# Attention in front of a mixture of experts: strided heads in 24 groups of 54 tokens instead of 32 groups of 36

## The chip, the core and the metric

The kernel runs on one core of one Trainium2 chip. The metric is device microseconds of one execution. In the profile PE is TensorE's matmuls, PEld its weight loads, DVE is VectorE, ACT is ScalarE, POOL is GpSimd and SP is SyncE, which issues most transfers here.

## What is computed

Attention over 4 batches, 8 heads, 576 tokens and 64 features per head, followed by a layer of eight experts and by a dense layer (512 to 2048 to 512, with an ELU between). The change touches the attention alone. Heads 0 to 3 look back over a window of 32 tokens; heads 4 to 7 are strided: a token sees the earlier tokens with the same remainder modulo 32.

```python
scores = scale * np.matmul(q, k.transpose(0, 1, 3, 2))
rel = pos[:, None] - pos[None, :]
mask_local = (rel >= 0) & (rel < stride)
mask_strided = (rel >= 0) & (pos[None, :] % stride == pos[:, None] % stride)
scores = np.where(masks[None, :, :, :], scores, -1000000000.0)
attn = np.exp(scores - np.max(scores, axis=-1, keepdims=True))
attn = attn / (np.sum(attn, axis=-1, keepdims=True) + 1e-09)
return np.matmul(attn, v).astype(np.float32)
```

Each of the 32 remainders has 18 tokens, so the tokens that can see each other are small sets, and tokens of several remainders share one block with a mask.

## The kernel before, in words

**Stages.** The attention runs in about the first 120 us; the matmuls of the first expert come in at its end. Then five planned expert jobs and the dense layer fill the rest of the span. Each engine runs its instructions in the order in which the program emits them (`manual_schedule`); the framework adds the waits that the data need, and a tile that reuses a buffer waits for everything that used the tile before it, transfers included.

**Turns.** The attention takes its heads in pairs. For each batch the order is `PAIRS = [2, 0, 3, 1]`: strided, local, strided, local, so that the sixteen pairs n = 0 to 15 alternate. A turn n of the loop at L1425 emits, in this order: `emit_S(n)` (scores, DVE's addition of the mask, DVE's maximum, POOL's subtraction, then `store_x`), the transposes of q and k of pair n + 1 (`emit_T`), `emit_PT(n - 1)` (transposes of the exponentials), more transposes, `emit_PV(n - 1)` (P times V, then DVE's product with the reciprocal sum into the x tile, L1330 for strided and L1358 and L1361 for local heads), `emit_X(n - 2)` (transposes of x, and ACT's copy into xt), after a batch's last pair `emit_L` and `emit_lg` (the router's logits), then `emit_exp(n)`, the loads of q and k of pair n + 3 and of V of pair n + 2. `bg()` places work of the first expert between them.

**Strided pairs.** A group holds 36 tokens: those of two remainders, 16 groups per head. PE multiplies 64 columns of q (36 of them used) with 36 tokens of k for a group in a quarter of its array, and writes eight slots of 36 scores for each half of the partitions and each head. A float32 matmul is two passes, so a pair has 64 of them for scores (L1246) and 64 for P times V (L1326), eight transposes of P (L1285) and eight of x (L1386). V is loaded by two transfers with rows of 2 KB (L1127).

**x tiles.** `x_sb` of a batch is one tile for its two strided pairs (`xs1`) and one for its two local pairs (`xs0`), each with one buffer (L1081). When the second pair of a kind is through (`pr % 2`), its stores to `x_dram` are appended to a list: two for a strided tile (L1338), three for a local one (L1365, 512 KB, and twice L1368, 32 KB). `store_x` at the end of `emit_S` empties the list onto POOL's queue. So the local stores of a batch are issued in turns 5, 9 and 13, and the next batch's first local pair writes the tile in turns 6, 10 and 14:

```python
    def store_x():
        while stores:
            stores.pop(0)()
```

PSUM tiles come from a function `bank` with a tag: S (scores, two banks), T (transposes of q and k, two), P (transposes of P, P times V and transposes of x, four). `idle` is a tile of zeros in bf16.

Of the kernel before, what the change touches and what calls it, by code (L numbers as in the profile page):

```python
# [24 lines left out]
M = 72  # L25
G = 8
J = 36
# [1044 lines left out]
def attention(tc, bg, q, k, v, mod, mbias, wg, x_dram, ident, router, bank):  # L1072
# [16 lines left out]
    vs = [const.tile([128, 2, G, D], F32, name=f"vs{i}") for i in range(2)]  # L1089
    vl = [const.tile([KW, 9, 2, D + 1], F32, name=f"vl{i}") for i in range(2)]  # L1090
    qt = [t_p.tile([128, S + 32], F32, name=f"qt{i}") for i in range(2)]

    kt = [t_p.tile([128, 32 + S], F32, name=f"kt{i}") for i in range(2)]
    sm_s = const.tile([128, 16 * D], F32, name="sm_s")
    sm_l = const.tile([128, 9, KW], F32, name="sm_l")
    pt_s = const.tile([128, 10 * D], F32, name="pt_s")
# [37 lines left out]

    mask_s = const.tile([128, J], F32, name="mask_s")
# [5 lines left out]
    def strided_mask():  # L1141
        di = const.tile([128, J], I32, name="di")
        nc.gpsimd.iota(di, pattern=[[-1, J]], base=64, channel_multiplier=1)
        nc.vector.tensor_scalar(di, di, 1, None, ALU.bitwise_and)
        nc.vector.tensor_copy(mask_s, di)
        nc.vector.tensor_scalar(mask_s, mask_s, NEG, None, ALU.mult)
        for x in range(2):
            sel(mask_s[64 * x:64 * x + 64], -1, ALU.is_ge, 0, 1)
# [17 lines left out]
    for t in qt:  # L1166
        nc.vector.memset(t[:, S:], 0.0)
    strided_mask()
    nc.vector.memset(sm_s, 0.0)
    nc.vector.memset(pt_s[:, S:], 0.0)  # L1170
# [46 lines left out]
    def emit_T(n, j):  # L1217

        b, pr = pairs[n]
        src = (qn if j < 2 else kn)[b, pr]  # L1220
        x = j % 2
        o = qt[n % 2][:, 0:S] if j < 2 else kt[n % 2][:, 32:]
        if pr >= 2:
            ps = bank("T", "ps_tr", 128, 3, 96)
            for c in range(3):
                nc.tensor.transpose(ps[:, c], src[:, 3 * x + c], ident[0:96, 0:96])
            nc.scalar.copy(o.rearrange("p (c w j) -> p c w j", w=2, j=J)[:, 4 * x:4 * x + 4], ps.rearrange("p x m -> p (x m)").rearrange("p (j w c) -> p c w j", w=2, c=4))
        else:
            ps = bank("T", "ps_tr", 128, 3, 96)
            for c in range(3):  # L1230
                nc.tensor.transpose(ps[:, c], src[:, 2 * c + x], ident[0:96, 0:96])
            nc.scalar.copy(o.rearrange("p (c m a) -> p c m a", c=3, a=2)[:, :, :, x], ps)

    def emit_S(n):
# [3 lines left out]
        if strided:  # L1238
            pss = [bank("S", f"ps_sc{r}", 128, 8, J) for r in range(2)]
            for i in range(8):  # L1240
                h, t, y = i // 4, i // 2 % 2, i % 2
                for x in range(2):
                    at = ((4 * h + 2 * x + t) * 2 + y) * J
                    for r in range(2):
                        ro = slice(D * r, D * r + D)
                        nc.tensor.matmul(pss[r][64 * x:64 * x + 64, i], lhsT=q_sb[ro, at:at + 64],  # L1246
                                         rhs=k_sb[ro, 32 + at:32 + at + J], start=True, stop=True)
            sm = sm_s.rearrange("p (s k) -> p s k", k=D)[:, :, 0:J]
            masks = [mask_s.unsqueeze(1).to_broadcast([128, 8, J])] * 2
            parts = [(0, 8), (8, 16)]  # L1250
        else:
            parts = [(0, TAIL + 1), (TAIL + 1, 9)]
            pss = [bank("S", f"ps_sl{r}", 128, TAIL + 1, KW) for r in range(2)]
            for s in range(TAIL + 1):
                for x in range(2):
                    for r in range(2):
                        if s == TAIL and r > x:
                            continue
                        blk = 64 * (2 * s + (x if s < TAIL else 0))
                        ro = slice(D * r, D * r + D)  # L1260
                        nc.tensor.matmul(pss[r][64 * x:64 * x + 64, s], lhsT=q_sb[ro, blk:blk + 64],
                                         rhs=k_sb[ro, blk:blk + KW], start=True, stop=True)
            sm = sm_l
            masks = [mask_l[:, i:j] for i, j in parts]
# [8 lines left out]
        store_x()  # L1273
# [5 lines left out]
    def emit_PT(n):  # L1279
        if pairs[n][1] >= 2:  # L1280
            sm, pt = sm_s, pt_s
            for r in range(2):
                ps = bank("P", "ps_p")
                for g in range(4):
                    nc.tensor.transpose(ps[:, 128 * g:128 * g + 128], sm[:, 512 * r + 128 * g:512 * r + 128 * g + 128], ident)  # L1285
                nc.scalar.copy(pt[:, 8 * J * r:8 * J * (r + 1)].rearrange("p (b q) -> p b q", q=J),
                               ps.rearrange("p (b q) -> p b q", q=D)[:, :, 0:J])
            rs = m_p.tile([128, 16], F32, tag="rs", name="rs")
# [4 lines left out]
            rec = m_p.tile([128, 2, 8], F32, tag="rec", name="rec")  # L1293
            nc.vector.reciprocal(rec.rearrange("p w (g r) -> p r g w", r=2), rs.rearrange("p (r g w) -> p r g w", r=2, w=2))
            bg()
            rss[n] = rec
            return
# [8 lines left out]
    xt = const.tile([128, 4, S], F32, name="xt")  # L1306

    def emit_PV(n):
# [4 lines left out]
        if key not in xs:  # L1313
            sh = [128, 8, 4, D] if strided else [128, 18, D]
            xs[key] = xs_p.tile(sh, F32, tag=f"xs{pr // 2}", name="xs")
        x_sb = xs[key]
        xb = x_dram[b * S:(b + 1) * S]
        if strided:
            pss = [bank("P", "ps_v", 128, 8, D) for w in range(2)]
            for g in range(8):  # L1320
                h, t, r = g // 4, g // 2 % 2, g % 2
                for x in range(2):
                    for w in range(2):
                        ro = slice(64 * w, 64 * w + J)
                        at = (8 * r + 4 * h + 2 * t + x) * J
                        nc.tensor.matmul(pss[w][64 * x:64 * x + 64, g], lhsT=pt_s[ro, at:at + 64],  # L1326
                                         rhs=vs[pr - 2][ro, h, 4 * x + 2 * t + r], start=True, stop=True)
            rec = rss.pop(n).rearrange("p w (h t) -> p w h t", h=2)
            for w in range(2):
                nc.vector.tensor_tensor(x_sb[:, 4 * w:4 * w + 4, h0:h0 + 2].rearrange("p t h d -> p h t d"),  # L1330
                                        pss[w].rearrange("p (h t) d -> p h t d", h=2),
                                        rec[:, w].unsqueeze(3).to_broadcast([128, 2, 4, D]), ALU.mult)
                bg()
                bg()
            if pr % 2:
                o = xb[:, 4 * D:].rearrange("(q w x t) d -> x q w t d", w=2, x=2, t=4)
                for x in range(2):
                    stores.append(lambda x=x: nc.gpsimd.dma_start(o[x], x_sb[64 * x:64 * x + J].rearrange("q (w t) h d -> q w t (h d)", w=2)))  # L1338
# [31 lines left out]
    def store_x():  # L1370
        while stores:
            stores.pop(0)()

    def emit_X(n):
# [4 lines left out]
        if n + 2 >= NP:  # L1379
            store_x()  # L1380
        if pr >= 2:
            for half in range(2):
                ps = bank("P", "ps_x")
                o = ps.rearrange("p (q x t) -> p t x q", x=2, t=4)
                for g in range(4):
                    nc.tensor.transpose(o[:, g], x_sb[:, 4 * half + g, h0:h0 + 2].rearrange("p h d -> p (h d)"), ident)  # L1386
                nc.scalar.copy(xt[:, pr].rearrange("p (q t) -> p q t", q=J)[:, :, 8 * half:8 * half + 8],
                               ps.rearrange("p (q t) -> p q t", t=8)[:, 0:J])
# [7 lines left out]
        nc.scalar.copy(xt[:, pr, 0:512], ps)  # L1396
        nc.scalar.copy(xt[:, pr, 512:S], pe)
# [3 lines left out]
    def emit_L(b):  # L1401

        for half in range(2):
            ps = bank("T", "ps_l", 128, S // 2)
            for kk in range(4):
                nc.tensor.matmul(ps[32 * kk:32 * kk + 32], lhsT=wgp[:, kk], rhs=xt[:, kk, half * (S // 2):(half + 1) * (S // 2)],
# [87 lines left out]
```

## Time and profile before

| | |
|---|---|
| median of three runs | 731.36 us (728.81 to 732.5) |
| the profiled execution's own time | 732.11 us |
| its span, first to last instruction | 730.4 us |
| mean granted clock of TensorE | 0.993 |
| transfers over the span | 127.36 MB, 174 GB/s |

Durations below come from the one profiled execution, whose time is 1.7 us above its span. A busy share is an average over stages that differ: the attention's is read from its own stretch. Idle time of an engine stands in brackets behind a row, with what ended it. Queue rows (PEldq, SPq) are of the sequencers.

### The profile page before, as it was taken

The page shows a single profiled execution, that of the slowest core. Times are in us where ns is not written, and L with a number is a line of the kernel's source. Part 1 is how long each engine was busy: PE and PEld are TensorE (multiplying, and loading weights), DVE is VectorE, ACT ScalarE, POOL GpSimd, SP SyncE. Part 2 cuts the span into 40 slices and gives each one's busy share as a digit, 9 for nine tenths or more (in the row PEclk, how much of TensorE's full clock was granted, in tenths as well). Part 3 has the DMA queues.
Part 4 walks back from the last instruction along what each step waited for, and adds up shares of the span by engine and source line. Part 5 has one row for each costly group of instructions (what it writes and reads, how often), then busy time and mean ns, then how long its engine had stood idle before and what let it go on. Part 6 is the DMA issues. An engine that isn't in the chain of part 4 may idle for free.

```text
span 730.4 us, 13943 instructions
## 1 busy us (share of the span) xinstructions
PE 711.9 (97%) x5263; PEld 626.1 (86%) x5266; DVE 555.0 (76%) x1068; ACT 415.9 (57%) x761; POOL 110.1 (15%) x164
## 2 busy tenths in 40 slices
PE   8899989999999999999999999999999999999996
PEld 5788876888888888888998998999889889899895
DVE  4668876967879877777878867787788898777763
ACT  5577775235544546455555546675565677565643
POOL 3444352121020200000000000021000003200003
PEclk9899999999999999999999999999999999999999
DMA  9988773177586686674865464165433345533302
GB/s 192 196 223 197 209 229 95 61 231 230 163 281 212 210 272 195 202 237 149 292 227 204 172 217 144 58 207 168 165 124 115 116 142 204 189 130 116 115 2 86
DMA packets 94983, 127.36 MB, mean 174 GB/s; under 512 B 19415, under 2 KB 66551, under 8 KB 94912
## 3 DMA queue, kind: packets, MB, share of 16 engines
q1 hardware_dynamic: 85440, 94.91, 42.7%
q0 software_dynamic: 9472, 31.51, 13.0%
q8 instruction: 43, 0.70, 0.4%
q14 instruction: 28, 0.23, 0.1%
HBM read 100.18 MB, written 26.21 MB: 173 GB/s over the span
## 4 chain that ended last, share of the span: by engine, by line
PE 51%; POOL 1%; issue 0%; POOLq 0%; ACT 0%
PE h_ps L719 25%; PE o_ps L810 9%; PE o_ps L809 9%; PE o_ps L808 9%; POOL out_dram L819 1%; POOLq L1490 0%; ACT y_sb L817 0%; POOLq L819 0%
## 5 line engine op out<-in xcount | busy, mean ns | idle before, releaser
L810 PE MATMUL o_ps<-wh,gl 128*128 128x512 f32 x282 | 111.2, 394 | 0.0
L809 PE MATMUL o_ps<-wl,gh 128*128 128x512 f32 x282 | 111.0, 394 | 0.0
L808 PE MATMUL o_ps<-wh,gh 128*128 128x512 f32 x282 | 110.6, 392 | 0.0
L794 ACT CAST gh<-t 128x384 fp32r<-128x384 f32 x94 | 48.3, 514 | 102.3 <-DVE t L746 100.3
L490 DVE TENSOR_TENSOR wl<-wraw,wh 128x1024 fp32r<-128x1024 f32 x56 | 69.0, 1232 | 32.4 <-ACT wh L489 31.9
L719 PE MATMUL h_ps<-xa,wh 128*128 128x384 f32 x320 | 87.6, 338 | 1.1 <-DVEq L756 0.6
L745 DVE SCALAR_TENSOR_TENSOR t<-e,t 128x384 f32<-128x384 f32 x96 | 53.4, 557 | 28.7 <-ACT e L740 26.3
L870 POOL DMA_DIRECT2D wl<-wl_dram x32 | 17.5, 551 | 338.1 <-PE o_ps L810 197.6
L719 PEld LDWEIGHTS h_ps<-xa,wh 128*128 128x128 f32 x320 | 59.3, 188 | 7.8 <-issue 1.6
L800 DVE TENSOR_TENSOR gl<-t,gh 128x384 fp32r<-128x384 f32 x94 | 52.2, 556 | 17.3 <-ACT gh L794 15.5
L719 PE MATMUL h_ps<-xa,wl 128*128 128x384 f32 x192 | 64.6, 336 | 0.0
L810 PEld LDWEIGHTS o_ps<-wh,gl 128*128 128x128 f32 x282 | 52.9, 188 | 12.0
L524 PE MATMUL y_ps<-hh,wh 128*128 128x460 f32 (+1 forms) x160 | 61.4, 384 | 0.0
L526 PE MATMUL y_ps<-hh,wl 128*128 128x460 f32 (+1 forms) x160 | 60.1, 375 | 0.0
L525 PE MATMUL y_ps<-hl,wh 128*128 128x460 f32 (+1 forms) x160 | 60.0, 375 | 0.0
L489 ACT CAST wh<-wraw 128x1024 fp32r<-128x1024 f32 x56 | 58.4, 1043 | 0.0
L809 PEld LDWEIGHTS o_ps<-wl,gh 128*128 128x128 f32 x282 | 53.0, 188 | 6.2
L808 PEld LDWEIGHTS o_ps<-wh,gh 128*128 128x128 f32 x282 | 53.0, 188 | 6.2
L147 ACT ACTIVATE conv<-conv 128x512 f32<-128x512 f32 x32 | 21.8, 681 | 58.8 <-DVE conv L159 58.6
L719 PE MATMUL h_ps<-xb,wh 128*128 128x384 f32 x192 | 54.6, 338 | 0.0
L874 ACT CAST wh<-wraw 128x1024 fp32r<-128x1024 f32 x48 | 50.1, 1043 | 0.0
L719 PE MATMUL h_ps<-xc,wh 128*128 128x384 f32 x192 | 49.3, 338 | 0.0
(270 smaller groups left out, 1589.2 us busy)
## 6 DMA issues: line engine op xcount, KB each, us to landing
wraw<-w_f SPq DMA_DIRECT2D x48, 512.0 KB
wraw<-in_moe_w_dram SPq DMA_DIRECT2D x80, 256.0 KB
wl<-wl_dram POOLq DMA_DIRECT2D x32, 512.0 KB, 4.4
conv<-in_moe_w_in_dram SPq DMA_DIRECT2D x16, 512.0 KB
conv<-in_moe_w_out_dram SPq DMA_DIRECT2D x16, 512.0 KB
w_f<-conv SPq DMA_DIRECT2D x32, 256.0 KB
wl_dram<-wl SPq DMA_DIRECT2D x16, 512.0 KB
qn<-in_q_dram SPq DMA_DIRECT2D x16, 288.0 KB
```

Source lines behind the costliest of these rows:

```text
L489: nc.scalar.copy(WH[i], raw)
L490: nc.vector.tensor_tensor(WL[i], raw, WH[i].bitcast(F32), ALU.subtract)
L524: nc.tensor.matmul(ps, lhsT=a, rhs=hh, start=f == 0, stop=False)
L525: nc.tensor.matmul(ps, lhsT=a, rhs=hl, start=False, stop=False)
L526: nc.tensor.matmul(ps, lhsT=b, rhs=hh, start=False, stop=f == NCH - 1)
L719: mm = lambda x, v, f, l: nc.tensor.matmul(ps, lhsT=x, rhs=v, start=f, stop=l, skip_group_check=on)
L745: nc.vector.scalar_tensor_tensor(t, e, 1.0, t, ALU.add, ALU.mult)
L800: nc.vector.tensor_tensor(gl, t, gh.bitcast(F32), ALU.subtract)
L808: nc.tensor.matmul(ps, lhsT=a, rhs=hi, start=first, stop=False)
L809: nc.tensor.matmul(ps, lhsT=a, rhs=lo, start=False, stop=False)
L810: nc.tensor.matmul(ps, lhsT=b, rhs=hi, start=False, stop=last)
L874: nc.scalar.copy(WH[slots(n)[nm]], wts[n, nm])
```

## The change

`J, R3, Z = 18, 3, 3`, `N3 = J * R3` = 54 and `Q6 = 2 * Z * N3` = 324 replace M, G and the old J. A group holds the tokens of three remainders, 12 groups per head; the last ones reach beyond 32 remainders and hold padding. Scores have six slots of 54 instead of eight of 36 for each head, P and x six slots instead of eight. V of a strided pair is loaded by six transfers of 18 rows each, in pieces of 512 bytes. After the transposes of a strided tile of q or k a matmul with two columns of zeros fills two columns that the copy reads as padding. The strided x tile gets two buffers, the local one keeps one (`bufs=1 + pr // 2`). A strided x tile is stored by six transfers, and `store_x` takes at most how many stores to issue. xt gets rows of 36 with 32 used. The mask is made by POOL alone, and unused rows of V are filled with zeros.

```diff
-M = 72
-G = 8
-J = 36
+J, R3, Z = 18, 3, 3
+N3 = J * R3
+Q6 = 2 * Z * N3
...
-            src = v[b, h:h + 2].rearrange("h (j w a) d -> w j h (a d)", w=2, a=G)
+            src = v[b, h:h + 2].rearrange("h (j c a) d -> h j c (a d)", c=16, a=2)
             for w in range(2):
-                nc.sync.dma_start(vs[pr - 2][64 * w:64 * w + J].rearrange("j h a d -> j h (a d)"), src[w])
+                for i in range(R3):
+                    n = min(6, 16 - 6 * i)
+                    ro = slice(64 * w + J * i, 64 * w + J * (i + 1))
+                    nc.sync.dma_start(vs[pr - 2][ro, 0:n, 0:2 * D], src[w, :, 6 * i:6 * i + n])
...
         if pr >= 2:
-            ps = bank("T", "ps_tr", 128, 3, 96)
+            ps = bank("T", "ps_tr")
             for c in range(3):
-                nc.tensor.transpose(ps[:, c], src[:, 3 * x + c], ident[0:96, 0:96])
-            nc.scalar.copy(o.rearrange("p (c w j) -> p c w j", w=2, j=J)[:, 4 * x:4 * x + 4], ps.rearrange("p x m -> p (x m)").rearrange("p (j w c) -> p c w j", w=2, c=4))
+                nc.tensor.transpose(ps[:, 96 * c:96 * c + 96], src[:, 3 * x + c], ident[0:96, 0:96])
+            nc.tensor.matmul(ps[:, 288:290], lhsT=idle[:, 0:128], rhs=idle[:, 0:2], start=True, stop=True)
+            o = qt[n % 2][:, Q6 * x:Q6 * x + Q6] if j < 2 else kt[n % 2][:, 32 + Q6 * x:32 + Q6 * x + Q6]
+            wide = bass.AP(ps.tensor, ps.offset, [list(ps.ap[0]), [1, 6], [6, R3], [16, J]])
+            nc.scalar.copy(o.rearrange("p (v i j) -> p v i j", i=R3, j=J), wide)
...
-            pss = [bank("S", f"ps_sc{r}", 128, 8, J) for r in range(2)]
-            for i in range(8):
...
+            pss = [bank("S", f"ps_sc{r}", 128, 6, N3) for r in range(2)]
+            for z in range(Z):
+                for h in range(2):
+                    for x in range(2):
+                        at = (6 * h + 3 * x + z) * N3
+                        for r in range(2):
+                            ro = slice(D * r, D * r + D)
+                            nc.tensor.matmul(pss[r][64 * x:64 * x + 64, 2 * z + h], lhsT=q_sb[ro, at:at + 64],
+                                             rhs=k_sb[ro, 32 + at:32 + at + N3], start=True, stop=True)
...
-        store_x()
+        store_x(3)
...
-                for g in range(4):
-                    nc.tensor.transpose(ps[:, 128 * g:128 * g + 128], sm[:, 512 * r + 128 * g:512 * r + 128 * g + 128], ident)
...
+                for z in range(Z):
+                    nc.tensor.transpose(ps[:, 128 * z:128 * z + 128], sm[:, 384 * r + 128 * z:384 * r + 128 * z + 128], ident)
...
-            sh = [128, 8, 4, D] if strided else [128, 18, D]
-            xs[key] = xs_p.tile(sh, F32, tag=f"xs{pr // 2}", name="xs")
+            sh = [128, 6, 4, D] if strided else [128, 18, D]
+            xs[key] = xs_p.tile(sh, F32, tag=f"xs{pr // 2}", bufs=1 + pr // 2, name="xs")
...
-            pss = [bank("P", "ps_v", 128, 8, D) for w in range(2)]
...
+            pss = [bank("P", "ps_v", 128, 6, D) for w in range(2)]
...
             for w in range(2):
...
+                nc.vector.tensor_tensor(x_sb[:, :, h0 + w], pss[w], rec[:, w].unsqueeze(2).to_broadcast([128, 6, D]), ALU.mult)
                 bg()
                 bg()
             if pr % 2:
-                o = xb[:, 4 * D:].rearrange("(q w x t) d -> x q w t d", w=2, x=2, t=4)
-                for x in range(2):
-                    stores.append(lambda x=x: nc.gpsimd.dma_start(o[x], x_sb[64 * x:64 * x + J].rearrange("q (w t) h d -> q w t (h d)", w=2)))
+                o = xb[:, 4 * D:].rearrange("(j c) d -> j c d", c=32)
+                for y in range(6):
+                    i, x = divmod(y, 2)
+                    cnt = min(6, 32 - 6 * y)
+                    stores.append(lambda y=y, cnt=cnt, at=64 * x + J * i: nc.gpsimd.dma_start(
+                        o[:, 6 * y:6 * y + cnt], x_sb[at:at + J, 0:cnt].rearrange("j s h d -> j s (h d)")))
             return
...
-    def store_x():
-        while stores:
+    def store_x(most):
+        for _ in range(min(most, len(stores))):
             stores.pop(0)()
...
         if n + 2 >= NP:
-            store_x()
+            store_x(len(stores))
```

## Rows read from the trace of the kernel before

**Rows 1.** The page: busy time, share of the span and instructions by engine.

```profile
PE 711.9 (97%) x5263; PEld 626.1 (86%) x5266; DVE 555.0 (76%) x1068; ACT 415.9 (57%) x761; POOL 110.1 (15%) x164
```

**Rows 2.** Stretches: length, busy PE, PEld, DVE, ACT, POOL; granted clock, DMA share, GB/s.

```profile
0.00:30.00 30.00, 24.72 (x400) 18.24 (x404) 12.59 (x33) 14.39 (x30) 13.16 (x41) 0.91 1.08 195
30.00:100.00 70.00, 67.29 (x1547) 57.86 (x1546) 54.55 (x145) 50.96 (x118) 32.95 (x44) 0.99 0.86 216
...
128.00:730.00 602.00, 595.61 (x3013) 531.33 (x3012) 468.30 (x849) 333.55 (x581) 56.82 (x71) 1.00 0.51 171
```

**Rows 3.** Timeline, PE's weight loads in turns 6 to 10: start, us, operation, count.

```profile
48.31 1.02 PEld L1246 LDWEIGHTS ps_sc<-kt,qt 64*64 64x64 f32 x64
...
52.70 0.86 PEld L1386 LDWEIGHTS ps_x<-ident,xs 128*128 128x128 f32 x8
...
55.18 0.88 PEld L1285 LDWEIGHTS ps_p<-ident,sm_s 128*128 128x128 f32 x8
...
56.73 1.02 PEld L1326 LDWEIGHTS ps_v<-vs,pt_s 36*64 36x64 f32 x64
...
77.22 0.35 PEld L266 LDWEIGHTS <-ones 128*128 128x128 bf16 x9
```

**Rows 4.** Groups by form, 5 to 128 us: busy us, mean ns; idle before, releaser.

```profile
L1330 DVE TENSOR_TENSOR xs<-ps_v,rec 128x512 f32<-128x512 f32 x16 | 10.5, 686 | 2.0 <-PE ps_l L1406 1.3
...
L1387 ACT COPY xt<-ps_x 128x288 f32<-128x288 f32 x16 | 6.4, 399 | 13.1 <-PE ps_x L1386 12.9
...
L1271 DVE TENSOR_REDUCE mx<-sm_s 128x16 f32<-128x576 f32 x8 | 6.0, 753 | 0.4
```

**Rows 5.** Timeline of POOL, turns 5 to 7.

```profile
46.47 0.82 POOL L1365 DMA_DIRECT2D x_dram<-xs  x1
47.28 1.23 POOL L1368 DMA_DIRECT2D x_dram<-xs  x2
51.28 1.15 POOL L1272 TENSOR_TENSOR sm_s<-sm_s,mx 128x576 f32<-128x576 f32 x1 [2.76 <-ACT pt_l L1302]
57.71 1.63 POOL L1272 TENSOR_TENSOR sm_l<-sm_l,mx 128x864 f32<-128x864 f32 x1 [5.28 <-DVE mx L1271]
```

**Rows 6.** Hardware queue, packets, MB, share: 0 to 110 us, then the whole span.

```profile
q1 hardware_dynamic: 37344, 17.83, 74.8%
...
q1 hardware_dynamic: 85440, 94.91, 42.7%
```

**Rows 7.** Timeline of DVE, first local x product in turns 6, 10, 14.

```profile
54.25 0.75 DVE L1358 TENSOR_TENSOR xs<-ps_v,rs 128x256 f32<-128x256 f32 x2 [0.92 <-DMA x_dram<-xs]
...
78.08 0.42 DVE L1358 TENSOR_TENSOR xs<-ps_v,rs 128x256 f32<-128x256 f32 x1
...
107.64 0.74 DVE L1358 TENSOR_TENSOR xs<-ps_v,rs 128x256 f32<-128x256 f32 x2
```

**Rows 8.** L1368's stores, issue to landing: 62 to 73 us, then 88 to 101.

```profile
DMA to landing us min/median/max: 5.6/5.7/5.9
...
DMA to landing us min/median/max: 4.0/4.2/4.5
```

**Rows 9.** Timeline of POOL, strided subtraction in turns 10 and 14.

```profile
76.79 1.16 POOL L1272 TENSOR_TENSOR sm_s<-sm_s,mx 128x576 f32<-128x576 f32 x1 [0.23 <-DVE mx L1271]
...
104.55 1.15 POOL L1272 TENSOR_TENSOR sm_s<-sm_s,mx 128x576 f32<-128x576 f32 x1 [3.65 <-DVE mx L1271]
```

**Rows 10.** Timeline of ACT, the local pair's exponentials of turn 7.

```profile
59.84 0.93 ACT L1277 ACTIVATE sm_l<-sm_l 128x864 f32<-128x864 f32 x1
```

**Rows 11.** Timeline of PE, its longest idle stretch behind 5 us.

```profile
25.14 0.48 PE L1345 MATMUL ps_v<-vl,pt_l 96*64 96x65 f32 x4 [2.87 <-issue]
```

**Rows 12.** Stretches of 2 us, columns as in rows 2.

```profile
24.00:26.00 2.00, 0.86 (x9) 0.74 (x10) 0.09 (x2) 0.00 (x0) 0.46 (x1) 0.59 1.03 196
...
30.00:32.00 2.00, 2.00 (x17) 2.00 (x16) 1.93 (x4) 1.22 (x4) 0.00 (x0) 0.70 1.03 188
```

More of the change, by code (lines that the diff above doesn't have):

```diff
@@ L1087, in attention @@
     NP = len(pairs)
-    vs = [const.tile([128, 2, G, D], F32, name=f"vs{i}") for i in range(2)]
+    vs = [const.tile([128, 6, 2 * D + 8], F32, name=f"vs{i}") for i in range(2)]
     vl = [const.tile([KW, 9, 2, D + 1], F32, name=f"vl{i}") for i in range(2)]
-    qt = [t_p.tile([128, S + 32], F32, name=f"qt{i}") for i in range(2)]
-    kt = [t_p.tile([128, 32 + S], F32, name=f"kt{i}") for i in range(2)]
-    sm_s = const.tile([128, 16 * D], F32, name="sm_s")
+    qt = [t_p.tile([128, n], F32, name=f"qt{i}") for i, n in enumerate((2 * Q6 + 10, S))]
+    kt = [t_p.tile([128, 32 + n], F32, name=f"kt{i}") for i, n in enumerate((2 * Q6, S))]
+    sm_s = const.tile([128, 12 * D], F32, name="sm_s")
     sm_l = const.tile([128, 9, KW], F32, name="sm_l")
-    pt_s = const.tile([128, 10 * D], F32, name="pt_s")
+    pt_s = const.tile([128, 2 * Q6 + 10], F32, name="pt_s")
     pt_l = const.tile([KW, 9, 128], F32, name="pt_l")
@@ L1141, in strided_mask @@
     def strided_mask():
[L1142 to L1146, printed above, removed]
+        nc.gpsimd.memset(mask_s, 0.0)
         for x in range(2):
-            sel(mask_s[64 * x:64 * x + 64], -1, ALU.is_ge, 0, 1)
+            o = mask_s[64 * x:64 * x + 64]
+            sel(o, -1, ALU.is_ge, 0, 1)
+            o = o.rearrange("p (i j) -> p i j", j=J)
+            nc.gpsimd.affine_select(o, o, pattern=[[J, R3], [0, J]], compare_op=ALU.is_ge, fill=NEG, base=J - 1, channel_multiplier=-1)
     def local_masks():
@@ L1165, in attention @@
     make_identity(nc, ident)
-    for t in qt:
-        nc.vector.memset(t[:, S:], 0.0)
+    nc.vector.memset(qt[0][:, 2 * Q6:], 0.0)
     strided_mask()
+    for t in vs:
+        nc.vector.memset(t[:, 4:6], 0.0)
     nc.vector.memset(sm_s, 0.0)
-    nc.vector.memset(pt_s[:, S:], 0.0)
+    nc.vector.memset(pt_s[:, 2 * Q6:], 0.0)
     load_v(*pairs[0])
@@ L1238, in emit_S @@
         if strided:
-            pss = [bank("S", f"ps_sc{r}", 128, 8, J) for r in range(2)]
-            for i in range(8):
-                h, t, y = i // 4, i // 2 % 2, i % 2
-                for x in range(2):
[L1243 to L1250, printed above, removed]
+            pss = [bank("S", f"ps_sc{r}", 128, 6, N3) for r in range(2)]
[7 more added lines that the diff above has]
+                                             rhs=k_sb[ro, 32 + at:32 + at + N3], start=True, stop=True)
+            sm = sm_s.rearrange("p (s k) -> p s k", k=D)[:, :, 0:N3]
+            masks = [mask_s.unsqueeze(1).to_broadcast([128, 6, N3])] * 2
+            parts = [(0, 6), (6, 12)]
         else:
@@ L1304, in attention @@
     xs, stores = {}, []
-    xt = const.tile([128, 4, S], F32, name="xt")
+    xt = const.tile([128, 4, J, 36], F32, name="xt")
     def emit_PV(n):
@@ L1318, in emit_PV @@
         if strided:
-            pss = [bank("P", "ps_v", 128, 8, D) for w in range(2)]
[L1320 to L1328, printed above, removed]
+            pss = [bank("P", "ps_v", 128, 6, D) for w in range(2)]
+            for z in range(Z):
+                for r in range(2):
+                    for x in range(2):
+                        for w in range(2):
+                            ro = slice(64 * w, 64 * w + N3)
+                            at = (6 * r + 2 * z + x) * N3
+                            nc.tensor.matmul(pss[w][64 * x:64 * x + 64, 2 * z + r], lhsT=pt_s[ro, at:at + 64],
+                                             rhs=vs[pr - 2][ro, 3 * x + z, D * r:D * r + D], start=True, stop=True)
+            rec = rss.pop(n)
             for w in range(2):
-                nc.vector.tensor_tensor(x_sb[:, 4 * w:4 * w + 4, h0:h0 + 2].rearrange("p t h d -> p h t d"),
-                                        pss[w].rearrange("p (h t) d -> p h t d", h=2),
-                                        rec[:, w].unsqueeze(3).to_broadcast([128, 2, 4, D]), ALU.mult)
+                nc.vector.tensor_tensor(x_sb[:, :, h0 + w], pss[w], rec[:, w].unsqueeze(2).to_broadcast([128, 6, D]), ALU.mult)
                 bg()
@@ L1379, in emit_X @@
         if n + 2 >= NP:
-            store_x()
+            store_x(len(stores))
         if pr >= 2:
[L1382 to L1388, printed above, removed]
+            for a in range(2):
+                ps = bank("P", "ps_x")[:, 0:384]
+                o = ps.rearrange("p (q x z) -> p z x q", x=2, z=Z)
+                for z in range(Z):
+                    nc.tensor.transpose(o[:, z], x_sb[:, 2 * z + a, h0:h0 + 2].rearrange("p h d -> p (h d)"), ident)
+                nc.scalar.copy(xt[:, pr].rearrange("p j (i u a) -> p a j i u", i=R3, a=2)[:, a],
+                               ps[:, 0:6 * N3].rearrange("p (i j u) -> p j i u", i=R3, u=6))
             return
@@ L1405, in emit_L @@
             for kk in range(4):
-                nc.tensor.matmul(ps[32 * kk:32 * kk + 32], lhsT=wgp[:, kk], rhs=xt[:, kk, half * (S // 2):(half + 1) * (S // 2)],
+                nc.tensor.matmul(ps[32 * kk:32 * kk + 32], lhsT=wgp[:, kk], rhs=xt[:, kk, half * (J // 2):(half + 1) * (J // 2), 0:32],
                                  start=True, stop=True)
```

19 lines of the change are left out of this document (9 added, 10 removed).

## The prediction, made before the changed kernel had run

> **What bounds the kernel now.** I read the page, then the stretches, then the timelines of the attention. The page gives TensorE (PE) 97% of the span [rows 1]. The table of stretches splits that: from 128 us on PE is busy 595.6 of 602 us, so whatever the attention gains or loses in front shifts that whole tail and the end with it; from 30 to 100 us it is busy 67.3 of 70, and DVE and ACT, at 54.6 and 51.0, have room; in the first 30 us PE loses 5 us while the DMA share is 1.08 [rows 2]. So the attention, sixteen turns n = 0 to 15 (even ones strided heads, odd ones local heads), is paced by PE, as long as nothing on DVE, POOL or a transfer makes PE wait. The profiled execution took 732.11 us for a span of 730.4; the median of the runs is 731.36, so I sum against 732.1 and take 0.75 off. A measurement of this kernel can tell about 0.5% (3.7 us) from no change.
>
> **PE, removed and added.** Each of the eight strided pairs goes from 8 to 6 slots. Scores: 64 matmul passes become 48. The weight loads of 64 passes with 36 columns take 1.02 us, and the 64 passes with 64 columns in P·V take 1.02 us as well [rows 3]: the price goes by count, not by columns, so 54 columns lie between two rows of one price, and both groups lose a quarter, 0.255 us each. Transposes of P and of x: 8 become 6, from 0.88 and 0.86 us [rows 3], 0.22 us each. Added: four matmuls with two bf16 columns, one per transposed tile. Nine such loads took 0.35 us [rows 3], so four cost 0.16. Per pair that is 0.945 - 0.16 = 0.79 us, over eight pairs **6.3 us** of PE work less. The Trainium skill, "TensorE: Matmul & The Clock Gate", § Step-by-step: what each phase is for, says that throughput is N cycles for N columns; by it scores would go from 64 x 36 to 48 x 54 columns, 12% longer instead of 25% shorter, and the eight pairs would give 3.2 us where the rows give 6.3. The two equal rows speak against it here.
>
> **ACT, DVE, POOL.** A score row set grows from 576 to 648 elements, an eighth. ACT copies of 399 ns [rows 4] grow to 449 at most, eight per pair, and exp by less than 0.1: 0.5 us per pair at most, hidden while ACT waits for PE (12.9 us at the x copies alone [rows 4]); without that cover, up to 4 us. DVE: the maximum, 753 ns [rows 4], and the sum each grow by 0.09, the two additions together by 0.1; the two final products lose a quarter of 686 ns [rows 4], 0.34: nothing net. POOL's subtraction, 1.15 us for 576 elements against 1.63 for 864 [rows 5], grows by 0.12. Mask and fills at the start lie in front of the first scores, while loads arrive; I cost them at nothing, half a microsecond if that cover is gone.
>
> **Loads and stores.** SP issues six V transfers per strided pair instead of two, 576 pieces of 512 bytes instead of 144 of 2 KB. The trace has no row for one piece, so I bound it by two rows: the hardware queue to 110 us (37344 packets, 17.83 MB, 74.8%) and the whole span (85440, 94.91 MB, 42.7%) [rows 6]. 16 x 110 x 0.748 / 37344 = 35 ns at 477 bytes; the rest of the span gives 76 ns at 1603 bytes; on the line through both, 512 bytes cost 36.5 ns and 2 KB 93. A pair's V then takes 21.0 us of engine time instead of 13.4, 0.5 us spread over sixteen engines. Loads run two or three pairs ahead and PE is busy at a share of 0.86 [rows 2], so I take 0; without that cover, 0.5 x 8 = 4 us. POOL issues 24 strided stores instead of 8, 0.6 to 0.8 us each [rows 5], 10 to 13 us on a queue that has room; they come behind the subtraction of their turn, and POOL's next one is a turn away. The strided x tile is now double, so these stores delay no writer.
>
> **The wait that decides.** The stores list is now drained three per turn. The strided pair's six go out in the next turn but one and the one after it; the local pair's three, appended last, therefore move one turn further: batch 0's go from turn 5 to turn 6. But the local x tile still has one buffer, and turn 6 is where batch 1's first local pair writes it (L1358). Today these stores follow the long subtraction and are issued at 46.47 and 47.28 us [rows 5], and even so L1358 starts at 54.25 after a wait of 0.92 us that a landing of x_dram ended [rows 7], 6.35 us after the last issue at 47.9. Moved, they follow turn 6's strided subtraction (51.28 + 1.15 + 0.12 = 52.55 [rows 5]); the last is issued 0.82 + 0.62 later, at 54.0. Issue to landing of the small stores was 5.7 in one batch and 4.2 in another [rows 8]; I take 5.7 under load, so 59.7: **5.4 us** after today's start (3.9 to 6.1). Batch 2: subtraction ends 76.79 + 1.16 + 0.12 [rows 9], last issue 79.5, landing 85.2 against a start at 78.08 [rows 7]: **7.1** (5.6 to 7.8). Batch 3: 104.55 + 1.15 + 0.12 [rows 9], last issue 107.3, landing 111.5 with that batch's 4.2 against 107.64 [rows 7]: **3.9**. Together 16.4 us. DVE runs in order: behind L1358 stand the next turn's score additions and maximum, then POOL's subtraction (57.71, 1.63 [rows 5]), ACT's exp (59.84 [rows 10]), then PE's transposes of P; PE also needs the PSUM banks and x that DVE holds. The chain has 0.5 us of slack, the gap between subtraction and exp; three times, that leaves **+14.9**.
>
> PE goes idle for 4 us or so in each. The trace has one idle stretch of this sort: after 2.87 us [rows 11] the granted clock shows 0.59, then reaches only 0.70 in the slice at 30 us [rows 12], about six microseconds near the lower level of 1.2 GHz, some 3 us of PE time. In the first two waits most of the slow time lies beside the DVE chain; I take 1.5 us each and nothing for the third, **+3** (0 to 9).
>
> Behind each wait the chain, not PE, sets the pace, so the savings of that turn's x, P and P·V work (about 0.8 us) are lost: of the 6.3 us, **-3.9** remain. The early idle stretch itself [rows 11] has no named releaser; with about 80 fewer PE instructions issued by then, PE gets further before it, and less is left for the slow clock. Its full price is 2.9 + 3 = 5.9; I take a third, **-2** (0 to -5.9).
>
> Sum: 14.9 + 3 - 3.9 - 2 = +12.0; 732.1 + 12.0 - 0.75 = **743.4 us**, 1.6% slower.
>
> **Rivals.** (1) Faster: PE's work alone counts, because the three waits fall where DVE and PE have room. For it: DVE waits several times for PE, and today's 0.92 us cost nothing visible. Against it: PE needs what stands behind L1358 within a turn. It decides only if the waits shrink below about 2 us each. 731.4 - 6.3 - 2 = 723. Chance 0.09. (2) No change: the stores land in 4.2 us (waits 3.9 + 5.6 + 3.9 - 1.5 = 11.9), the clock stays up, all 6.3 us are kept and the early stretch goes (5.9): 731.1. Each part is possible, all together are not likely; with half-measures around it, 0.15. (3) V comes late: in the first 30 us the DMA share is above 1 [rows 2], and V of pairs 0, 2 and 4 passes there. If each holds back the loads queued after it by the whole 0.5 us (7.7 us more of engine time over sixteen engines), or by 1.0 where only eight engines carry it, 1.5 to 3 us join the forecast: 745 to 746.4. For it: that share. Against it: the q and k loads are issued two turns ahead, and PE shows no wait for them. Chance 0.06. The Trainium skill, "DMA: Bandwidth & Descriptors", § Why a DMA increments its semaphore by 16 and not by 1, has a transfer use the largest number of engines up to sixteen that divides its slowest dimension, which is twelve for 36 rows and nine for 18. By it a V load would take 1.2 us longer on those nine (64 x 36.5 against 12 x 93 ns), 3.7 us for three; no row here shows which engines ran.
>
> **How the numbers follow.** The forecast keeps 0.70, from 737 (731.4 + 11.9 - 3.9 - 2: short landings, no clock loss) to 751 (731.4 + 16.6 + 9 - 3.9 - 2: long landings, three clock losses). Slower 0.70 + 0.06 = 0.76, same 0.15, faster 0.09. The range 732 to 751 leaves out rival 1, about half of rival 2's lower side and a little at the top, 0.2 together.
>
> **What would show it.** Right: L1358's counterpart idle 4 to 7 us "<- DMA x_dram" in turns 6, 10 and 14, PE idle in the same stretches, a lower granted clock after them; 48 passes for scores and P·V at about 0.77 us. Wrong: these waits absent or under 2 us, DMA named before PE's q, k or V matmuls, or score passes that cost more with 54 columns.

## The result, and the profile after

The changed kernel took 740.63 us (median of 4 runs, 738.9 to 741.61), the kernel before 731.81 beside it (728.81 to 732.5). The ratio is 1.0126, 95% interval 1.0090 to 1.0162: 1.3% slower, where 1.6% was forecast. The profiled execution took 739.77 us for a span of 738.0.

The page of the changed kernel, busy time by engine, answers to [rows 1]:

```profile
PE 712.9 (97%) x5007; PEld 626.2 (85%) x5010; DVE 553.7 (75%) x1066; ACT 416.5 (56%) x761; POOL 120.4 (16%) x182
```

Its stretches, columns as in [rows 2]:

```profile
0.00:30.00 30.00, 26.02 (x466) 19.38 (x470) 17.27 (x39) 18.62 (x40) 16.46 (x50) 1.00 0.96 191
30.00:100.00 70.00, 62.87 (x1186) 53.34 (x1185) 48.26 (x136) 45.32 (x105) 31.88 (x44) 0.90 0.89 205
100.00:128.00 28.00, 21.25 (x292) 17.00 (x288) 15.57 (x32) 15.60 (x31) 12.91 (x16) 0.88 0.42 117
```

PE has 256 instructions fewer and nearly the same busy total (712.9 us against 711.9). From 30 to 100 us it stood idle for longer than before and ran at a lower granted clock, 0.90 against 0.99 [rows 2], and every other engine is less busy there than before too. That is the mark of a wait that all of them share.

The timeline of DVE names it, at the first local x product of turns 6, 10 and 14 (L1365, L1358 before) [rows 7]:

```profile
52.47 0.76 DVE L1365 TENSOR_TENSOR xs<-ps_v,rs 128x256 f32<-128x256 f32 x2 [5.36 <-DMA x_dram<-xs]
...
81.75 0.42 DVE L1365 TENSOR_TENSOR xs<-ps_v,rs 128x256 f32<-128x256 f32 x1 [6.16 <-DMA x_dram<-xs]
...
114.93 0.76 DVE L1365 TENSOR_TENSOR xs<-ps_v,rs 128x256 f32<-128x256 f32 x2 [3.03 <-DMA x_dram<-xs]
```

And the timeline of POOL in turn 6 shows where the stores went (L1372 and L1375 are L1365 and L1368 of before) [rows 5]:

```profile
45.21 1.27 POOL L1278 TENSOR_TENSOR sm_s<-sm_s,mx 128x648 f32<-128x648 f32 x1 [3.08 <-PE ps_tr L1236]
46.43 0.82 POOL L1372 DMA_DIRECT2D x_dram<-xs  x1
47.23 1.23 POOL L1375 DMA_DIRECT2D x_dram<-xs  x2
```

Before, the local stores stood behind the long local subtraction of turn 5, five microseconds ahead of the strided one of turn 6; now they stand behind the latter. The store rows end at 48.46, and DVE is released at 52.47. The view of L1375's stores in that stretch has the difference; a landing is the moment when a transfer's data has arrived:

```profile
DMA to landing us min/median/max: 4.3/4.4/4.5
```

A store's row on POOL is thus not the store. The Trainium skill, "Perfetto Trace Analysis", § DMA Instruction — SWDGE (GPSIMD), says so: for DMAs that POOL issues, the profiler's end is when the last descriptor has been generated, not when the data has moved. The trace agrees: rows of 0.6 us, landings 4.4 us after the issue.

What the three waits cost is read from the start of each turn's exponential on ACT, one per turn, since every turn runs through it. The kernel before, turns 6, 10, 11, 14 and 15 (turn 7 is [rows 10]):

```profile
54.13 0.69 ACT L1277 ACTIVATE sm_s<-sm_s 128x576 f32<-128x576 f32 x1
...
78.93 0.69 ACT L1277 ACTIVATE sm_s<-sm_s 128x576 f32<-128x576 f32 x1
84.63 0.93 ACT L1277 ACTIVATE sm_l<-sm_l 128x864 f32<-128x864 f32 x1
...
106.32 0.69 ACT L1277 ACTIVATE sm_s<-sm_s 128x576 f32<-128x576 f32 x1
113.62 0.92 ACT L1277 ACTIVATE sm_l<-sm_l 128x864 f32<-128x864 f32 x1 [1.03 <-POOL sm_l L1272]
```

The changed kernel, turns 6, 7, 10, 11, 14 and 15:

```profile
47.74 0.75 ACT L1283 ACTIVATE sm_s<-sm_s 128x648 f32<-128x648 f32 x1
57.60 0.92 ACT L1283 ACTIVATE sm_l<-sm_l 128x864 f32<-128x864 f32 x1 [0.46 <-POOL sm_l L1278]
...
76.28 0.75 ACT L1283 ACTIVATE sm_s<-sm_s 128x648 f32<-128x648 f32 x1
87.36 0.92 ACT L1283 ACTIVATE sm_l<-sm_l 128x864 f32<-128x864 f32 x1 [0.62 <-POOL sm_l L1278]
...
110.00 0.76 ACT L1283 ACTIVATE sm_s<-sm_s 128x648 f32<-128x648 f32 x1
121.17 0.94 ACT L1283 ACTIVATE sm_l<-sm_l 128x864 f32<-128x864 f32 x1
```

At turn 6 it is 54.13 - 47.74 = 6.39 us ahead. The step from turn 6 to 7 takes 9.86 us instead of 5.71 (+4.15), from 10 to 11 11.08 instead of 5.70 (+5.38), from 14 to 15 11.17 instead of 7.30 (+3.87): 13.4 us lost in three places. Between them it loses half a microsecond more (-0.41 and +0.95). -6.39 + 13.40 + 0.54 = +7.55, and the spans differ by 7.6: from turn 15's exponential to the end both take 616.8. The whole difference between these two executions lies in these rows.

### The profile page after: what moved, and what is told of

Read it like the earlier page. It is cut to its first block, busy times and chain, and to the rows that moved or that the text cites. A ratio compares the mean times of both kernels' runs of the same rounds, so it can differ in the third digit from the quotient of the medians.

```text
span 738.0 us, 13498 instructions
## 1 busy us (share of the span) xinstructions
PE 712.9 (97%) x5007; PEld 626.2 (85%) x5010; DVE 553.7 (75%) x1066; ACT 416.5 (56%) x761; POOL 120.4 (16%) x182
## 4 chain that ended last, share of the span: by engine, by line
PE 51%; POOL 1%; issue 0%; POOLq 0%; ACT 0%
PE h_ps L719 25%; PE o_ps L810 9%; PE o_ps L809 9%; PE o_ps L808 9%; POOL out_dram L819 1%; POOLq L1497 0%; ACT y_sb L817 0%; POOLq L819 0%
```

## The experiments

Each ratio is against the kernel before on the same chip. Three chips took part; the kernel before had medians of 731.3, 736.6 and 730.9 us on them. The ratios are not the quotients of the two medians and differ from them by up to 0.2%; differences in us are worked out from the ratios.

**A second local x tile.** One number in the changed kernel:

```diff
-            xs[key] = xs_p.tile(sh, F32, tag=f"xs{pr // 2}", bufs=1 + pr // 2, name="xs")
+            xs[key] = xs_p.tile(sh, F32, tag=f"xs{pr // 2}", bufs=2, name="xs")
```

> The changed kernel with a second buffer of the local x tile, nothing else: L1365 can no longer wait for a store of x. Theory (the late local stores block the one local x tile): the three waits on DMA x_dram (14.5 us) and the three stretches of half clock after them (from 81.9 to 92 us, and two shorter ones) go, and the saving of PE work stays: 731.8 - 6.3 = 725.5, or down to 719.6 if the early idle stretch of PE stays away as well (another 5.9). So 719 to 726. Rival (V in small pieces, or the new PE work itself, holds PE back, and the stores are only what came last): other waits take the place of the three and the time stays at 736 to 741.

Measured: 728.35 us, ratio 0.9969 (0.9945 to 0.9993). The wait is gone altogether: the view of L1365 lists no idle time. Against the changed kernel that is 1.0126 / 0.9969 = 1.0157, 11.5 us (8.3 to 14.7) for the waits and what follows from them. The rival falls. But 728.35 is above the 719 to 726 that were expected: the groups of 54 bring about 2.3 us (0.5 to 4.0) here, not 6.3.

**All stores at once.** The old rule, one local tile:

```diff
-        store_x(3)
+        store_x(len(stores))
```

> The changed kernel with the old rule for the stores: each turn issues all that stand in the list, so the local stores go one turn earlier again; the local x tile keeps its one buffer. Theory (it is the turn in which they are issued): the local stores have a whole turn more, L1365 waits under 1 us each time, 719 to 727, within 2 us of the kernel with two local tiles; six strided stores at once cost POOL about 4 us in a turn in which it has room. Rival (it is the small stores' number and their transfers, 24 instead of 8, that make the x stores land late): the waits stay above 2 us each and the time above 733.

Measured: 729.27 us, ratio 0.9987 (0.9958 to 1.0017). L1365 waits 0.3 us in all, and the time is within 1 us of two local tiles, as the theory has it; only its level was again missed. The size and number of the new stores make no difference that these runs can tell; the turn does.

**The kernel before, with only the stores moved.** Four empty places hold the local stores back by a turn; `store_x` takes at most three, as in the change.

```diff
+                stores.extend([lambda: None] * 4)
...
-        store_x()
+        store_x(3)
```

> The kernel before with three stores per turn and four empty places behind the two strided stores of a batch, so that the local stores go out in the same turn as in the changed kernel (turns 6, 10, 14); groups, V, tiles and PE work as before. Theory: the wait alone makes the loss: L1358 waits about 5, 7 and 4 us for x_dram, a low granted clock follows each, and the time is 742 to 750 (731.8 plus 14.9, less up to 5 where the chain has more slack, plus up to 3 of clock), longer than the changed kernel, which has 6.3 us less PE work and no early idle stretch. Rival (V or the new work does it): 730 to 734.

Measured: 749.79 us (744.67 to 753.45), ratio 1.0232 (1.0187 to 1.0278). The old groups, V and PE work, and L1359 (L1358 of before) waits 15.2 us in three places. Its exponentials, turns 6, 7, 10, 11, 14 and 15:

```profile
51.92 0.69 ACT L1277 ACTIVATE sm_s<-sm_s 128x576 f32<-128x576 f32 x1
61.87 0.93 ACT L1277 ACTIVATE sm_l<-sm_l 128x864 f32<-128x864 f32 x1
...
81.78 0.69 ACT L1277 ACTIVATE sm_s<-sm_s 128x576 f32<-128x576 f32 x1
93.38 0.92 ACT L1277 ACTIVATE sm_l<-sm_l 128x864 f32<-128x864 f32 x1 [2.10 <-POOL sm_l L1272]
...
115.66 0.69 ACT L1277 ACTIVATE sm_s<-sm_s 128x576 f32<-128x576 f32 x1
126.47 0.94 ACT L1277 ACTIVATE sm_l<-sm_l 128x864 f32<-128x864 f32 x1
```

The three steps take 9.95, 11.60 and 10.81 us, 4.24 + 5.90 + 3.51 = 13.7 more than before: the same price as the 13.4 in the changed kernel. So the moved stores are enough to make the whole loss, and the rest of the change is not needed for it. The ratio stands for 17.0 us (13.7 to 20.3), so the steps alone only just reach it. This execution ends 21.4 us later than before (751.8 against 730.4), though its attention is only 126.47 - 113.62 = 12.9 behind; the other 8.5 lie in the feed-forward part, where between 350 and 400 us PE is busy 44.43 of 50, 3.9 us of it waiting for one ACT conversion. Why that came late was not tried; the fastest of its four runs, 744.67, is 13.3 us above the median of before and has no room for it.

**V in 512-byte pieces, in the kernel before.** Its V tile gets a pitch that keeps the pieces apart, and eight transfers of 72 pieces:

```diff
-                nc.sync.dma_start(vs[pr - 2][64 * w:64 * w + J]..., src[w])
+                for i in range(4):
+                    ro, hh = 18 * (i // 2), i % 2
+                    nc.sync.dma_start(vs[pr - 2][64 * w + ro:64 * w + ro + 18, hh, :, 0:2 * D], src[w, ro:ro + 18, hh])
```

> The kernel before with V of the strided heads in 512-byte pieces, eight transfers of 72 pieces (18 rows) per pair instead of two of 72 pieces of 2 KB; nothing else changed. Theory (V is in time whatever its pieces): 730 to 734, at most the 4 us that the eight pairs' extra transfer time would cost if none were hidden. Rival (V comes late): PE waits for DMA v in the first turns, 736 or more.

Measured: 731.67 us, ratio 1.0003 (0.9982 to 1.0024). The pieces cost nothing, within 1.8 us.

**The second tile for the local pair instead of the strided one.** The same memory as the change, given to the other tile:

```diff
-... bufs=1 + pr // 2, name="xs")
+... bufs=2 - pr // 2, name="xs")
```

> The changed kernel with the second buffer given to the other tile: two local x tiles, one strided x tile; the same memory. Theory (only the local tile's stores come too late; the strided ones go out in turns 4 and 5 and the tile is written again in turn 7): as with two of each, 728.4, so 726 to 730, and no wait of L1336 or L1365 for x_dram above 1 us. Rival (with 24 small stores the strided tile needs its second buffer): L1336 waits above 2 us for x_dram and the time is above 731.

Measured: 740.57 us, ratio 1.0063 (1.0033 to 1.0093). The theory fell here, by an error in my reading of the code: the strided tile is written again in turn 5, by P·V of pair 4, not in turn 7, and with three stores per turn its last three are issued in that same turn. DVE's waits show it:

```profile
DVE xs L1336 <- DMA x_dram<-xs: 19.8, 3, 7.1
```

With three stores per turn in the order of the change, both tiles need the second buffer. The change gave one to the strided tile only.

**The kernel before with two local tiles**, a control:

> The kernel before with a second local x tile and nothing else. Theory (the 0.92 us that L1358 waits there costs nothing, so the 3 us by which the changed kernel with two local tiles beats the kernel before come from the groups of 54): 730 to 733. Rival (those 3 us are the tile's, and the groups bring nothing): 727 to 729.

Measured: 735.45 against 736.62 us, ratio 1.0001 (0.9979 to 1.0023). The 0.92 us of [rows 7] cost nothing that can be told, within 1.7 us; what the versions without the wait gain comes from the rest of the change, the groups.

**Filling PE's gaps.** Two local tiles, and in turns 12, 13 and 14:

```diff
+        if n in (12, 13, 14):
+            keep_busy(4)
         if n >= 1:
             emit_PV(n - 1)
```

> The changed kernel with two of each x tile, and four idle matmuls more ahead of P times V in turns 12, 13 and 14, where PE stood 1.6 us at 80 us and then ran at half clock to 87. Theory (the half clock after such gaps takes back a part of the 6.3 us, and filling them keeps the clock): granted clock 1.00 from 80 to 100 us, 724 to 727. Rival (the gap is the chain's, or PE has no room there: twelve matmuls of 0.2 to 0.45 us are 2.6 to 5.4 us): 728 to 733.

Measured: 733.63 against 736.62 us, ratio 0.9959 (0.9926 to 0.9992). The stretch at a lower clock does not come in this execution. From 84 to 88 us, first with two local tiles, then filled:

```profile
84.00:88.00 4.00, 4.00 (x76) 3.69 (x72) 2.60 (x7) 2.30 (x7) 3.08 (x4) 0.73 1.07 328
```

```profile
84.00:88.00 4.00, 3.39 (x64) 2.62 (x67) 2.87 (x10) 1.51 (x5) 2.57 (x4) 1.00 0.73 197
```

The ratio is 0.1% below that without filling, inside both intervals, and the two are from different chips: no gain can be told. Nor is it shown that the filling kept the clock: in the profile of all stores at once, and in the second one of the version that follows, neither of them filled, the clock is 1.00 from 84 to 88 us as well. This run decides nothing.

**The local stores first.** One local tile, three stores per turn, another order:

```diff
-            stores.append(lambda: nc.gpsimd.dma_start(o, x_sb[:, 0:16]...))
+            stores.insert(0, lambda: nc.gpsimd.dma_start(o, x_sb[:, 0:16]...))
...
-                stores.append(lambda r=r: ...)
+                stores.insert(1 + r, lambda r=r: ...)
```

> The changed kernel, one local tile, three stores per turn as it stands, but the local pair's three stores put at the head of the list, ahead of the three strided ones still in it: only the order differs. Theory (the turn in which the local stores are issued decides): L1365 waits under 1 us in turns 6, 10 and 14, 727 to 731. Rival (any x store still in flight blocks, whatever its place): waits above 2 us, 735 to 741.

Measured: 732.34 against 736.62 us, ratio 0.9933 (0.9908 to 0.9958). Once more, on another chip:

> The kernel with the local stores first once more, beside the next three on one chip: 0.990 to 0.996 of the kernel before. It is the base that those three change.

727.33 against 730.91, ratio 0.9962 (0.9937 to 0.9987). POOL's timeline of that run, turns 5 and 6:

```profile
39.63 0.83 POOL L1372 DMA_DIRECT2D x_dram<-xs  x1
40.46 1.25 POOL L1375 DMA_DIRECT2D x_dram<-xs  x2
44.76 1.27 POOL L1278 TENSOR_TENSOR sm_s<-sm_s,mx 128x648 f32<-128x648 f32 x1 [3.05 <-PE ps_tr L1236]
45.98 1.85 POOL L1344 DMA_DIRECT2D x_dram<-xs  x3
```

The local stores are issued at 39.63 instead of 46.43, and L1365 waits 0.9 us in all, once. The same tiles, transfers and matmuls, and the order of one list is worth 0.4 to 0.7% against the kernel before and 1.6 to 1.9% against the change. This is the version that beats both.

**The price of the two-column matmuls.** Each of the 32 issued four times:

```diff
+            for _ in range(4):
-            nc.tensor.matmul(ps[:, 288:290], lhsT=idle[:, 0:128], rhs=idle[:, 0:2], start=True, stop=True)
+                nc.tensor.matmul(ps[:, 288:290], lhsT=idle[:, 0:128], rhs=idle[:, 0:2], start=True, stop=True)
```

> The local stores first, and each of the 32 two-column matmuls issued four times, 96 more: their price by addition. By the price of the prediction (39 ns each, from nine weight loads in a row) 3.7 us more than the base; by the 0.10 us that each of their weight loads shows in the changed kernel's trace, 9.6 us more; hidden beside the other work: less than 1.5 us more. The theory behind the missing gain takes the second: then the 32 cost 3.2 us of the 6.3.

Measured: 727.49 against 730.91, ratio 0.9955 (0.9932 to 0.9978). Against its base that is -0.07% (-0.41 to +0.27), so at most about 2 us for 96. My theory falls, and the price of the prediction with it. Its weight loads, all 128 of them:

```profile
L1230 PEld LDWEIGHTS <-idle 128*128 128x128 bf16 x128 | 7.5, 97 | 0.0
```

7.5 us against 3.1 for the 32 of the base: 4.4 us of weight loads went in, and at most 2 us came out in the time. A rival stays open: in these single executions the granted clock is 1.00 from 72 to 120 us with the added matmuls, and 0.57 from 108 to 112 us in the base, so they may have paid for a part of themselves.

**The two columns filled by ACT instead.**

```diff
-            nc.tensor.matmul(ps[:, 288:290], lhsT=idle[:, 0:128], rhs=idle[:, 0:2], start=True, stop=True)
+            nc.scalar.copy(ps[:, 288:290], zero)
```

> The local stores first, and the 32 two-column matmuls replaced by a copy of two zero columns on ACT, which has room (7.5 of 10 us). Theory (each tiny matmul costs PE 0.10 us in a stretch that PE paces): 2 to 3.5 us less than the base. Rival (they lie beside the wait for the copy that follows): within 1 us of the base; and if ACT's extra 32 copies of about 0.2 us stand on the way from the transposes to the scores, up to 6 us more.

Measured: 730.17 against 730.91, ratio 0.9984 (0.9964 to 1.0004), 0.22% above its base (-0.10 to +0.54). No gain; if anything the second half of the rival. The new copies come one by one on ACT, each ahead of the copy that reads its two columns:

```profile
60.80 0.17 ACT L1231 COPY ps_tr<-zero 128x2 f32<-128x2 f32 x1 [0.34 <-PE ps_tr L1230]
61.00 0.43 ACT L1234 COPY qt<-ps_tr 128x324 f32<-128x324 f32 x1
```

**The same with two local tiles.**

> The last one with a second local x tile as well. Theory (with the stores first the local tile's buffer is no longer waited for): within 1.5 us of the one before it. Rival (the 0.7 us that L1365 still waits, and stores that land late, matter): 1.5 to 4 us faster.

Measured: 729.36 us, ratio 0.9982 (0.9962 to 1.0002): the same as the one before it, so with the stores first the second buffer is not needed.

## Why the prediction was right, and where its sum was off

**The wait that decides: right, in place and nearly in size.** Predicted at L1358's counterpart in turns 6, 10 and 14: 5.4, 7.1 and 3.9 us of delay, 16.4 in all. Measured waits: 5.36, 6.16 and 3.03, 14.5. The 5.4 counts from a start that had itself waited 0.92 us [rows 7], so what compares with 16.4 is 14.5 - 0.9 = 13.6. Too long was the landing: 5.7 us were taken for the first two and 4.2 for the third, and 4.4, 4.3 and 3.9 came. The slack of 0.5 us each did not come out that evenly: 4.44 us of added wait cost 4.15, 6.16 cost 5.38, and 3.03 cost 3.87, more than the wait. In sum 13.6 cost 13.4. That the stores' turn makes the wait is shown from four sides: the control with only the stores moved, the two versions that issue them a turn earlier, and the two tiles.

**The clock term: mis-sized.** +3 us was taken, for PE idle for 4 us or so in each wait. PE's longest idle stretches there were 2.99, 1.97 and 3.98 us, and the low clock came all three times, longer than assumed. Stretches of 2 us, one behind the first wait, two behind the second, one behind the third:

```profile
54.00:56.00 2.00, 2.00 (x60) 1.60 (x55) 1.93 (x4) 0.29 (x1) 0.06 (x1) 0.64 1.33 205
...
82.00:84.00 2.00, 1.31 (x46) 1.32 (x46) 2.00 (x8) 0.00 (x0) 0.00 (x0) 0.50 0.40 115
...
90.00:92.00 2.00, 2.00 (x21) 1.77 (x21) 1.90 (x8) 1.53 (x4) 0.49 (x1) 0.50 0.90 295
...
116.00:118.00 2.00, 1.74 (x36) 1.30 (x40) 1.89 (x5) 0.59 (x1) 0.00 (x0) 0.50 0.00 0
```

From 82 to 92 us PE ran at the lower level of 1.2 GHz. The first half of that lies ahead of turn 11's exponential (87.36), in a step that grew by less than its wait, 5.38 against 6.16. The second half lies in turns 11 to 14, which took 110.00 - 87.36 = 22.64 us, against 22.23 in the second run of the version with the local stores first (76.76 to 98.99), whose clock is 1.00 there: 0.4 us more. DVE is busy for 2.00 of 2 us at 82, and what paces these turns seems to run through DVE, with PE catching up beside it. The prediction said this for its first two waits and priced it at 1.5 us each; it is nearly nothing. For the third wait it took nothing, and there the step grew by 0.84 us more than the wait, with the clock at 0.50 from 116 to 122 us; whether that is the clock's price was not separated.

**The PE terms: one row wrong, and the premise too strong.** Of the passes the trace shows what was predicted: 48 score passes in 0.79 us (the timeline of weight loads has 70.26, 0.79 x48) against 1.02 for 64 [rows 3], 16 ns each or little more, whether of 36, 54 or 64 columns. The Trainium skill's rule of N cycles for N columns, weighed in the prediction ("TensorE: Matmul & The Clock Gate", § Step-by-step: what each phase is for), would have made them longer; the measurement decides against it for these passes. What was missed is the transposes of q and k, the changed kernel's weight loads at turn 9:

```profile
63.52 0.28 PEld L1228 LDWEIGHTS ps_tr<-ident,qn 96*128 96x128 f32 x3
63.74 0.10 PEld L1229 LDWEIGHTS <-idle 128*128 128x128 bf16 x1
63.83 0.29 PEld L1228 LDWEIGHTS ps_tr<-ident,qn 96*128 96x128 f32 x3
64.05 0.10 PEld L1229 LDWEIGHTS <-idle 128*128 128x128 bf16 x1
64.14 0.64 PEld L1291 LDWEIGHTS ps_p<-ident,sm_s 128*128 128x128 f32 x6
```

From 63.52 to 64.14 they take 0.62 us; in the kernel before, the six in a row run from 65.92 to 66.40, 0.48. That is 0.07 us per tiny matmul, not 0.04, and leaves 0.945 - 0.28 = 0.67 us per pair, 5.3 over eight, instead of 6.3. But that does not explain the measured gain of the versions without the wait either: 2.3 us with two local tiles, 1.0 with all stores at once, 4.9 and 2.8 with the local stores first. Nor would it have helped to know: 4.4 us of weight loads added changed the time by 2 us at most. What failed is the first paragraph of the prediction, "the attention is paced by PE". PE busy 67.3 of 70 us [rows 2] counts matmul records that overlap and are modelled to their ends, and there is room in it, at least where q and k are transposed.

Single executions do not settle how much of a saving arrives. From turn 4's exponential to turn 10's, three strided pairs, the old groups take 38.05 us (40.88 to 78.93), 38.29 with two local tiles and 39.20 with V in small pieces; the new ones without the waits take 36.48 and 36.85 with the local stores first, 37.06 with two local tiles and 37.75 with all stores at once. Three pairs' PE saving at 0.67 us is 2.0; the means differ by 1.5, and the two executions of one kernel by 0.4. With 96 tiny matmuls more it is 37.33, with the ACT copies 37.88 and 37.61: too near to say what those cost. That the turn is a chain through PE, ACT and DVE, in which work of each counts in part, would fit all this, and is not shown.

**The early idle stretch: gone, but not for the reason given, and worth nothing at the median.** A third of it (-2 us) was credited to the change, since fewer PE instructions stand ahead of it. In the changed kernel it is absent, which looked like a full gain of 5.9. The timelines of PE of three versions with the old groups answer to [rows 11]: only the stores moved, then two local tiles, then V in small pieces. Up to turn 4 the first two are the program of the kernel before.

```profile
21.14 1.04 PE L1346 MATMUL ps_v<-vl,pt_l 96*64 96x65 f32 x28
23.11 0.34 PE L1346 MATMUL ps_v<-vl,pt_l 96*64 96x65 f32 x4 [0.94 <-issue]
```

```profile
21.01 1.04 PE L1345 MATMUL ps_v<-vl,pt_l 96*64 96x65 f32 x28
23.52 0.34 PE L1345 MATMUL ps_v<-vl,pt_l 96*64 96x65 f32 x4 [1.47 <-issue]
```

```profile
22.19 1.15 PE L1347 MATMUL ps_v<-vl,pt_l 96*64 96x65 f32 x32
```

In all three profiles with V in pieces of 2 KB the gap sits behind the same 28th matmul, 2.87 us before and 0.94 and 1.47 here. In all eleven with pieces of 512 bytes, old groups or new, there is none. The granted clock from 14 to 36 us is 0.84, 0.92 and 0.94 in the three, and 1.00 in the eleven. So it goes with the loads of V and not with the number of PE instructions; why is open. Its size varies by execution. And it was worth nothing that the median shows: V in small pieces alone, which removes it, made a ratio of 1.0003, a gain of 1.3 us at most with whatever the pieces themselves cost. In its profile it is 54.13 - 50.12 = 4.0 us ahead of the kernel before at turn 6 and 0.1 at turn 15 (113.53). The other two are 0.9 and 2.2 us ahead at turn 6, so of the changed kernel's lead of 6.39 us there, a part belongs to the one profiled execution of before.

**What was costed at nothing.** V: confirmed, 1.0003 (0.9982 to 1.0024). POOL's subtraction: 1.27 us, as worked out (1.15 + 0.12). DVE's maximum: 0.83 against 0.753, as worked out. ACT's copies take 430 to 459 ns by group; the bound was 449. The 24 stores: POOL spent 14.9 us issuing them, against 6.1 for 8, so 8.8 more where 10 to 13 were predicted, and they cost nothing that can be told once they were in the right order.

**The sum in one line.** Predicted 14.9 + 3 - 3.9 - 2 = +12.0. By the runs: the three steps with the waits +13.4, the clock behind them about +0.4, groups about -3 (the mean of 2.3, 1.0, 4.9 and 2.8), the early stretch 0: +10.8; measured +9.2 (6.6 to 11.9). Waits and clock were put 4.1 us too high and the two gains 2.9 too high as well, so the errors cancelled in part: that the total came this near is to that extent luck.

**The rivals.** (1), PE's work alone: the shortest of the three waits was 3.03 us and its step grew by 3.87, so the 2 us below which this rival decides were not reached. (2), no change: short landings did come (4.4, 4.3 and 3.9, where it asked for 4.2), the clock cost little and the early stretch did go; but that stretch was worth nothing at the median, and about half of the 6.3 us arrived. (3), V late: no PE wait for V, ratio 1.0003.

## What to carry to other kernels

Where a list of deferred transfers is drained a few at a time, its last entries move to a later turn, and whoever rewrites their source waits: check for every tile in the list in which turn it is written next, and order the list by that. A second buffer helps only the tile that gets it, and two tiles were late in the order of the change; changing the order of the list needs no memory and did as much. And before a high busy share is called the pace, add some work to that engine: 4.4 us of weight loads more on an engine "96% busy" cost 2 us at most.

## What the runs showed of the hardware beside that

In one execution DVE, ACT and PE stood still together while POOL issued gathers. In the first run with the local stores first, timelines of POOL, DVE and ACT early in turn 13:

```profile
88.22 0.95 POOL L467 DMA_INDIRECT xg<-x_dram,idx  x1 [0.30 <-issue]
89.48 0.95 POOL L467 DMA_INDIRECT xg<-x_dram,idx  x1 [0.30 <-issue]
```

```profile
89.86 1.12 DVE L1274 TENSOR_TENSOR sm_l<-ps_sl,mask_l 128x480 f32<-128x480 f32 x2 [4.34 <-remote]
```

```profile
91.29 0.76 ACT L1232 COPY qt<-ps_tr 128x324 f32<-128x324 f32 x2 [5.57 <-remote]
```

The matmuls that DVE and ACT read from had ended at 86.14 and 86.85 us, so both had their operands for 3.7 and 4.4 us of their idle 4.3 and 5.6; PE stood 4.2 behind ACT. The granted clock was 0.58 from 92 us and then 0.50 until 104. From turn 12's exponential to turn 13's took 14.2 us, and 7.8 in the other run of the same kernel. Together with the early gap behind one matmul (2.87, 0.94 and 1.47 us in three executions that are one program up to there), this is where executions of one program here differ by several microseconds. Whether it is the fetching of instructions, which the page of the profile lists as a queue of its own (41 transfers, 0.67 MB in the changed kernel), was not tried.
